# Token mixing by 26 block products on one core: the sums of z a product ahead of their high parts, weight parts four steps ahead in five buffers, gates and biases moved forward

## The chip, the cores and the metric

The kernel runs on one core of a Trainium2 chip. A core has a matrix engine (PE, with weight loads shown apart as PEld), a vector engine (DVE), an activation engine (ACT), a general engine (POOL) and a queue that issues the transfers here (SP). Each engine works through its own list of instructions in order, and waits by semaphores for the others. The metric is the device time of one execution in microseconds (us).

## The reference, cut to what matters

A block of attention is followed by a gated MLP whose gate mixes the 2048 tokens with a 2048 x 2048 matrix. The change lies in the second part:

```python
h = _layernorm(x, axis=-1) * (1 + cb) + sb
z = _gelu(jnp.einsum("bsd,df->bsf", h, w_in))
z1 = z[..., :Fh]
z2 = _layernorm(z[..., Fh:], axis=-1)
g = jnp.einsum("ts,bsf->btf", w_sp, z2) + b_sp[None, :, None]
x = x + gb * jnp.einsum("bsf,fd->bsd", z1 * g, w_out)
```

There are 2048 tokens, 448 channels, and 896 features in each of z1 and z2. Everything is float32.

## The kernel before, in words

The stages follow each other: queries, keys and values; attention over 16 heads; the output projection; z1 and z2; the mixing (the einsum with w_sp); and the last projection with w_out. A float32 product is made of three PE passes on float32r operands: each operand is split into a high part (a copy with rounding, on ACT) and a low part (operand minus high part, on DVE), and high times high, high times low and low times high are summed in PSUM.

**Mixing.** z2 lies in SBUF as four groups of tokens, each with two halves of the features: B is the first 384, A the other 512 (384 and 128). w_sp transposed is cut into 4 x 4 blocks of 512 x 512. In place of 32 block products there are 26 (the table PRODUCTS), each of a sum of z blocks with a sum of weight blocks; its result is added to or subtracted from the output tiles that its row of signs names. Sixteen products are 512 features wide, ten are 384 wide (flag `six`). A product n has four steps (n, 0) to (n, 3), one for each 128 tokens of its group; the list `mix` has the 104 steps. `mix_step` issues 12 matmuls a step for a wide product and 9 for a narrow one, all with 512 columns. Products with even n accumulate in one set of PSUM banks, odd ones in the other.

Around the matmuls each engine has work, and the loop at the end of the function sets its order, step by step:

- `w_load` (SP): brings the raw weight block of a step, 128 x 512, into a tile `raw_sp`. The sums of blocks were made during the attention and lie in DRAM (`ws_scr`); twelve loads come straight from the input.
- `w_split`: the weight's high part `wsp_h` (ACT) and low part `wsp_l` (DVE) of step i + 3, at the start of step i. `raw_sp`, `wsp_h` and `wsp_l` have four buffers each, so the high part of step i + 3 takes the buffer that step i - 1 has used.
- `z_begin(n + 2)` in step (n, 1): the sum of z blocks for product n + 2 (DVE, `z_op`), where there is one, and then its high part (ACT, `z_hi`). `z_end(n + 2)` in step (n, 3): its low part (DVE, `z_low`). The parts lie in `heapA`, in three buffers.
- `read_list(n - 1)`: when product n - 1 is done, its banks are added into the output tiles cE, cC, cF and cD (group k = 0 to 3, tile f = 0 to 6 of 128 features each), at most three at a step: DVE adds, or an ACT copy for the first one of a tile.
- `extra`: work placed by hand with `put` and `gates`. `bias` adds b_sp (POOL), `z1_load` brings a tile of z1 (SP, two buffers), `gate` multiplies by it (POOL; DVE for a few later), `u_split` splits a finished tile for the last projection (ACT and DVE). `wout_load` (SP, two buffers `raw_out`), and `wout_part` (POOL, then ACT and DVE) prepare w_out. `x2_load` brings rows for the last sum.

After the last step come 16 calls of `y_part`, each with 21 matmuls with 448 columns: the last projection.

In the trace, instructions of the shared helper `sub` have line 141, reads, biases and gates (`d_add`) line 1392, the matmuls of the mixing line 1384, weight loads line 1164, z1 loads line 1424 and w_out loads line 1442. The name z stands for z2 and for z1's tiles, cD and so on for the output tiles.

## Time and profile before

| | us |
|---|---|
| median of 3 runs | 1406.65 (1404.82 to 1407.26) |
| the profiled execution's own time | 1407.99 |
| its span, first to last instruction | 1406.1 |
| first and last matmul of the mixing start at | 1050.7 and 1334.1 |
| PE busy, share of the span | 98% |

The 1.9 us between the span and the execution's own time lie outside the instructions. A matmul's record is longer than the time by which the next one follows it, because matmuls are pipelined; so PE reads as busy even where it is slowed, and the number of matmuls that start in a stretch tells more than the share of busy time. The mixing has 1128 matmuls: 420 in products 0 to 9, 528 in products 10 to 21, 180 in products 22 to 25.

### The profile page before, as it was taken

Reading aid. Unit: us, or ns where it says so; the run is one execution under the profiler, and the core shown is the slowest. Engines: PE = TensorE matmul, PEld = TensorE weight load, DVE = VectorE, ACT = ScalarE, POOL = GpSimd, SP = SyncE. Lnnn points to the kernel's source line nnn. Section 1 sums busy time; section 2 is a strip of 40 time slices with the busy share of each in tenths; the row PEclk is TensorE's granted clock in tenths of the full one; section 3 lists DMA queues with packets and bytes.
Section 4 is the critical chain, followed back from the end, with each engine's and each line's share of the span. In section 5 each row is a group of like instructions: output and inputs, shape, how many; then the busy total and the mean of one; then the engine's idle time right before and its main releaser. Section 6 shows DMA issues by size and latency. Waiting matters only on the chain. (4 is left out here: it accounts for less than half of the span.)

```text
span 1406.1 us, 20080 instructions
## 1 busy us (share of the span) xinstructions
PE 1384.8 (98%) x7120; PEld 978.5 (70%) x7120; DVE 1073.5 (76%) x1685; ACT 785.3 (56%) x1458; POOL 427.2 (30%) x394
## 2 busy tenths in 40 slices
PE   9999999999999999999999999999999999998899
PEld 8888655555555555555555556988987788776698
DVE  7798888888888888888888842840477689889661
ACT  5623677666777777666777787452235543343230
POOL 2234334233345336434510021100240014136600
PEclk9999999999999999999999999999999999999999
DMA  8564642455244543553233002532003333344442
GB/s 268 144 178 177 183 123 79 116 161 160 63 121 129 165 113 119 156 147 85 98 98 81 17 22 81 191 126 104 28 9 120 105 111 121 120 128 143 149 149 92
DMA packets 89008, 168.12 MB, mean 120 GB/s; under 512 B 16584, under 2 KB 27978, under 8 KB 86362
## 3 DMA queue, kind: packets, MB, share of 16 engines
q1 hardware_dynamic: 86190, 162.54, 38.5%
q10 hardware_dynamic: 2718, 4.30, 0.8%
q8 instruction: 56, 0.92, 0.3%
q14 instruction: 44, 0.36, 0.1%
HBM read 108.40 MB, written 53.60 MB: 115 GB/s over the span
## 5 line engine op out<-in xcount | busy, mean ns | idle before, releaser
L696 DVE TENSOR_REDUCE pm<-mt 128x1 f32<-128x512 f32 x1024 | 631.7, 682 | 86.1 <-PE mt L691 86.0
L727 ACT ACTIVATE P<-st_ps 128x512 f32<-128x512 f32 x1024 | 514.5, 627 | 201.2 <-PE st_ps L723 201.1
L723 PE MATMUL st_ps<-qst,kst 128*128 128x512 f32 x1024 | 404.3, 406 | 0.0
L691 PE MATMUL mt<-kst,qst 128*128 128x512 f32 x1024 | 402.0, 393 | 0.5 <-DMA qst<-qk_scr 0.5
L723 PEld LDWEIGHTS st_ps<-qst,kst 128*128 128x128 f32 x1024 | 191.2, 188 | 140.3 <-issue 93.1
L738 PE MATMUL o_ps<-P,V 128*32 128x512 f32 x2048 | 247.1, 598 | 0.0
L1384 PE MATMUL acc<-wsp_h,heapA 128*128 128x512 f32 x752 | 239.4, 397 | 6.9 <-ACT wsp_h L1170 3.5
L845 POOL TENSOR_TENSOR ws_raw<-ws_raw 128x512 f32<-128x512 f32 x124 | 159.2, 1287 | 192.8 <-DMA ws_scr<-ws_raw 128.6
L691 PEld LDWEIGHTS mt<-kst,qst 128*128 128x128 f32 x1024 | 192.4, 188 | 33.8 <-issue 0.9
L1384 PEld LDWEIGHTS acc<-wsp_h,heapA 128*128 128x128 f32 x752 | 143.3, 191 | 42.3 <-ACT wsp_h L1170 7.0
L1384 PE MATMUL acc<-wsp_l,heapA 128*128 128x512 f32 x376 | 150.0, 399 | 7.9 <-DVE wsp_l L141 7.8
L738 PEld LDWEIGHTS o_ps<-P,V 128*32 128x32 f32 x2048 | 54.7, 109 | 121.7 <-issue 113.7
L141 DVE TENSOR_TENSOR wsp_l<-raw_sp,wsp_h 128x512 fp32r<-128x512 f32 x104 | 88.1, 864 | 47.0 <-ACT wsp_h L1170 47.0
L1170 ACT ACTIVATE wsp_h<-raw_sp 128x512 fp32r<-128x512 f32 x104 | 62.0, 627 | 77.1 <-PE acc L1384 43.7
L1384 PEld LDWEIGHTS acc<-wsp_l,heapA 128*128 128x128 f32 x376 | 71.8, 191 | 28.3 <-DVE wsp_l L141 14.0
L1203 ACT ACTIVATE heapA<-z 128x1536 fp32r<-128x1536 f32 (+2 forms) x25 | 33.7, 1359 | 54.9 <-DVE z L1193 53.3
L380 PE MATMUL pq<-heapD,heapD 128*128 128x512 f32 x196 | 61.9, 390 | 0.0
L767 POOL TENSOR_TENSOR osb<-osb,rb 128x512 f32<-128x512 f32 x15 | 19.3, 1288 | 122.1 <-DMA rb<-r_scr 112.4
L1282 DVE BATCH_NORM_STATS2 stz<-z 128x6 f32<-128x448 f32 x32 | 20.0, 626 | 46.3 <-ACT z L1281 25.9
L1281 ACT ACTIVATE z<-z_ps 128x448 f32<-128x448 f32 x32 | 17.4, 545 | 47.2 <-PE z_ps L1278 47.2
L1392 POOL TENSOR_TENSOR cE<-cE,bt 128x512 f32<-128x512 f32 x7 | 12.2, 1767 | 99.1 <-DVE cE L1392 99.1
L141 DVE TENSOR_TENSOR heapA<-z,heapA 128x1536 fp32r<-128x1536 f32 (+2 forms) x25 | 42.0, 1689 | 0.0
(219 smaller groups left out, 1520.4 us busy)
## 6 DMA issues: line engine op xcount, KB each, us to landing
ws_scr<-ws_raw SPq DMA_DIRECT2D x92, 256.0 KB
raw_sp<-ws_scr SPq DMA_DIRECT2D x92, 256.0 KB
ws_raw<-in_w_spT_dram SPq DMA_DIRECT2D x72, 256.0 KB
kst<-qk_scr SPq DMA_DIRECT2D x45, 224.0 KB
qst<-qk_scr SPq DMA_DIRECT2D x45, 224.0 KB
qk_scr<-qh SPq DMA_DIRECT2D x28, 256.0 KB
qk_scr<-ql SPq DMA_DIRECT2D x28, 256.0 KB
z_scr<-z1t SPq DMA_DIRECT2D x28, 256.0 KB
```

The lines of the kernel that those rows point to most:

```text
L141: eng.tensor_tensor(out=dst, in0=a, in1=hi.bitcast(F32), op=ALU.subtract)
L380: pe.matmul(pq, wqk[:, b, m * 128 : (m + 1) * 128], hT[g][:, a, :], start=j == 0, stop=j == NST - 1)
L691: pe.matmul(mt, qst[h % 3][:, t * 128 : (t + 1) * 128], kst[h % 3][:, kb * 512 : (kb + 1) * 512], start=True, stop=True)
L696: dve.tensor_reduce(out=pms[h][:, t, kb : kb + 1], in_=mt, axis=AX.X, op=ALU.max)
L723: pe.matmul(st, kst[h % 3][:, kt * 128 : (kt + 1) * 128], qst[h % 3][:, qb * 512 : (qb + 1) * 512], start=True, stop=True)
L727: act.activation(p, st, AF.Exp, scale=SCALE)
L738: pe.matmul(otile[h][32 * qb : 32 * qb + 32, :], V[:, kt, h, :], ptiles.pop((u, qb)), start=kt == 0, stop=kt == NT - 1)
L845: pool.tensor_tensor(out=ws_tile(op[0]), in0=ws_tile(op[2]), in1=ws_tile(op[4]), op=ALU.add if op[3] == "+" else ALU.subtract)
L1170: act.activation(hi, raw, AF.Copy)
L1203: act.activation(zhi[n % 3][:, :, c], s, AF.Copy)
L1282: dve.bn_stats(out=st[:, hf, :], in_=z2[t][:, hf * D : (hf + 1) * D])
L1384: pe.matmul(a[j], z[:, c], w, start=start and k == 0, stop=st == 3 and k == 2, skip_group_check=not new or j == 3)
```

## The change

Seven things are changed, all in the mixing; the arithmetic and the number of instructions of each kind stay.

1. `z_begin` is taken apart. The sum for product n + 3 (`z_sums`) is made in step (n, 3), the high part of product n + 2 (`z_his`) in step (n, 1), its low part (`z_los`) in step (n, 2). Before, sum and high part were made in (n, 1), the low part in (n, 3).
2. `w_split` is taken apart. In step i, `w_hi(i + 4)` comes first on ACT, and `w_lo(i + 4)` comes last on DVE, behind the reads, the z work and the extras of the step. `wsp_h` and `wsp_l` get five buffers, `raw_sp` keeps four. `w_load(i + 6)` stands in place of i + 5. Four steps are ready before the mixing begins, before it three.
3. Two of the sums made by `put` stand two or three steps earlier.
4. The biases are moved forward: group 3 from products 14 to 15 to products 13 to 14, group 2 from 18 and 22 to 15 and 16, group 1 from 20 and 24 to 17 and 18, and their loads with them.
5. The gates of group 1 move from product 25 to 24; those of group 0, tiles 3 to 6, stand two steps earlier, those of tiles 0 to 2 about a step earlier or later. The splits of group 3's tiles 0 to 2 move from product 22 to 21.
6. z1 of group 3, tiles 3 to 6, and the rows of w_out get a tile `late_in` with four places in the old `heapB`; before, they shared pools with two buffers.
7. The rows of w_out are loaded from (23, 0) to (24, 3) in place of (22, 1) to (24, 1); `wout_part` runs from (23, 3) to (25, 1) in place of (23, 1) to (25, 1).

The order of instructions on DVE, where the program makes the sum of product 17 (`zt_sum`), in products 14 to 16; heapA rows are low parts of z, cF rows are reads. Before:

```order
L141 TENSOR_TENSOR wsp_l<-raw_sp,wsp_h 128x512
L1392 TENSOR_TENSOR cF<-cF,acc 128x512 x3
L141 TENSOR_TENSOR wsp_l<-raw_sp,wsp_h 128x512
L1193 TENSOR_TENSOR zt_sum<-zt_sum,z_10936 128x4x384
L1392 TENSOR_TENSOR cF<-cF,acc 128x512
L141 TENSOR_TENSOR wsp_l<-raw_sp,wsp_h 128x512 x2
L141 TENSOR_TENSOR heapA<-zt_sum,heapA 128x4x384
L141 TENSOR_TENSOR heapA<-z_10936,heapA 128x4x128
L141 TENSOR_TENSOR wsp_l<-raw_sp,wsp_h 128x512
L1392 TENSOR_TENSOR cF<-cF,acc 128x512 x3
```

With the change:

```order
L141 TENSOR_TENSOR wsp_l<-raw_sp,wsp_h 128x512
L1194 TENSOR_TENSOR zt_sum<-zt_sum,z_10936 128x4x384
L141 TENSOR_TENSOR wsp_l<-raw_sp,wsp_h 128x512
L1397 TENSOR_TENSOR cF<-cF,acc 128x512 x3
L141 TENSOR_TENSOR wsp_l<-raw_sp,wsp_h 128x512
L1397 TENSOR_TENSOR cF<-cF,acc 128x512
L141 TENSOR_TENSOR wsp_l<-raw_sp,wsp_h 128x512
L141 TENSOR_TENSOR heapA<-zt_sum,heapA 128x4x384
L141 TENSOR_TENSOR heapA<-z_10936,heapA 128x4x128
L141 TENSOR_TENSOR wsp_l<-raw_sp,wsp_h 128x512 x2
```

The sum stands before the three reads in place of behind them, the low part of z a step earlier, and the weight's low parts stand at the end of the steps. On ACT the high part of `zt_sum` keeps its place among the high parts of the weights.

SP's transfers in products 22 to 24 (z_ rows are z1 tiles, raw_sp the weights of the mixing, raw_out and late_in the rows of w_out or z1). Before:

```order
L1442 DMA raw_out<-in_w_out_dram 128x448
L1164 DMA raw_sp<-ws_scr 128x512
L1442 DMA raw_out<-in_w_out_dram 128x448
L1164 DMA raw_sp<-ws_scr 128x512
L1424 DMA z_13374<-z_scr 128x512
L1164 DMA raw_sp<-ws_scr 128x512
L1424 DMA z_13398<-z_scr 128x512
L1442 DMA raw_out<-in_w_out_dram 128x448
L1164 DMA raw_sp<-ws_scr 128x512
L1424 DMA z_13423<-z_scr 128x512
L1442 DMA raw_out<-in_w_out_dram 128x448
L1164 DMA raw_sp<-ws_scr 128x512
```

With the change:

```order
L1164 DMA raw_sp<-ws_scr 128x512
L1436 DMA z_13403<-z_scr 128x512
L1454 DMA late_in<-in_w_out_dram 128x448
L1164 DMA raw_sp<-ws_scr 128x512
L1454 DMA late_in<-in_w_out_dram 128x448
L1164 DMA raw_sp<-ws_scr 128x512
L1436 DMA z_13453<-z_scr 128x512
L1454 DMA late_in<-in_w_out_dram 128x448
L1164 DMA raw_sp<-ws_scr 128x512
L1436 DMA z_13477<-z_scr 128x512
L1454 DMA late_in<-in_w_out_dram 128x448
L1164 DMA raw_sp<-ws_scr 128x512
```

Before, the rows of w_out share two buffers, and the third one stands ahead of a weight load; now they go to four places, later in the list, with a weight load between each two of them.

The diff:

```diff
--- before.py
+++ after.py
@@ -1157,20 +1157,21 @@
     raws, wsp = {}, {}
 
     def w_load(i):
-        if i < len(mix) and i not in raws and i not in wsp:
+        if i < len(mix):
             n, st = mix[i]
             raws[i] = wp.tile([128, 512], F32, name="raw_sp")
             b = PRODUCTS[n][3]
             sp.dma_start(raws[i], ws_scr[4 * n + st] if b is None else w_block(b, st))
 
-    def w_split(i):
-        if i < len(mix) and i not in wsp:
-            raw = raws.pop(i)
-            hi = wp.tile([128, 512], F32R, name="wsp_h")
-            act.activation(hi, raw, AF.Copy)
-            lo = wp.tile([128, 512], F32R, name="wsp_l")
-            sub(dve, lo, raw, hi)
-            wsp[i] = (hi, lo)
+    def w_hi(i):
+        if i < len(mix):
+            wsp[i] = [wp.tile([128, 512], F32R, name="wsp_h", bufs=5)]
+            act.activation(wsp[i][0], raws[i], AF.Copy)
+
+    def w_lo(i):
+        if i < len(mix):
+            wsp[i].append(wp.tile([128, 512], F32R, name="wsp_l", bufs=5))
+            sub(dve, wsp[i][1], raws.pop(i), wsp[i][0])
 
     zt = [dpool.tile([128, 8 * 896], F32, name=f"z2{i}", tag=f"heapD{i}") for i in range(2)]
     z2 = [zt[i // 8][:, i % 8 * FH : (i % 8 + 1) * FH] for i in range(NT)]
@@ -1255,13 +1256,15 @@
         24: lambda: [(C3, ZB[1])],
     }
 
-    def z_begin(n):
+    def z_sums(n):
         for s in SUMS[n]() if n in SUMS else ():
             z_op(*s)
+
+    def z_his(n):
         if n in HIS:
             z_hi(n, *HIS[n]())
 
-    def z_end(n):
+    def z_los(n):
         if n in HIS:
             z_low(n)
 
@@ -1291,15 +1294,15 @@
         dve.tensor_scalar(out=z2[t], in0=z2[t], scalar1=mv[:, 0:1], scalar2=rs, op0=ALU.subtract, op1=ALU.mult)
 
     early_z = {
-        5: lambda: z_begin(0),
-        6: lambda: z_end(0),
+        5: lambda: z_his(0),
+        6: lambda: z_los(0),
         8: zt_new,
         9: lambda: z_op(ZT[0], ZT[0], ZB[0]),
         10: lambda: z_op(ZT[0], ZT[0], ZB[1]),
-        11: lambda: z_begin(1),
-        12: lambda: z_begin(2),
-        13: lambda: z_end(2),
-        14: lambda: z_end(1),
+        11: lambda: z_his(1),
+        12: lambda: z_los(1),
+        13: lambda: z_his(2),
+        14: lambda: z_los(2),
         15: lambda: z_op(ZT[0], ZB[1], ZB[2]),
     }
     for t in range(NT + 1):
@@ -1307,10 +1310,12 @@
             z2_gemm(t)
         if 0 < t <= NT:
             z2_norm(t - 1)
-        if t in (10, 11, 13, 15):
-            w_load((10, 11, 13, 15).index(t))
-        if t in (13, 15, 16):
-            w_split((13, 15, 16).index(t))
+        if 9 <= t < 13:
+            w_load(t - 9)
+        if 12 <= t < 16:
+            w_hi(t - 12)
+        if 13 <= t < 17:
+            w_lo(t - 13)
         if t in early_z:
             early_z[t]()
     ph4.close()
@@ -1410,17 +1415,24 @@
         else:
             d_add(u, u, a, ALU.add if r > 0 else SUB)
 
-    bt, z1s = {}, {}
+    bt, z1s, ring2 = {}, {}, []
 
     def b_load(k):
         bt[k] = t4.tile([128, 512], F32, name="bt")
         sp.dma_start(bt[k], b_sp[k * 512 : (k + 1) * 512].rearrange("(o n) -> o n", o=1).broadcast_to([128, 512]))
 
-    def z1_load(f, k, late=False):
-        if late:
+    def late_tile(i):
+        if not ring2:
+            ring2.append(fh.tile([128, 4, 512], F32, name="late_in", tag="heapB"))
+        return ring2[0][:, i, :]
+
+    def z1_load(f, k, late=0):
+        if late == 0:
+            z1s[f, k] = t4.tile([128, 512], F32, name="z1")
+        elif late == 1:
+            z1s[f, k] = late_tile(f - 3)
+        else:
             z1s[f, k] = wp.tile([128, 512], F32, name="z1l", tag="raw_sp")
-        else:
-            z1s[f, k] = t4.tile([128, 512], F32, name="z1")
         sp.dma_start(z1s[f, k], z1_scr[f * 128 : (f + 1) * 128, k * 512 : (k + 1) * 512])
 
     def bias(f, k, eng=pool):
@@ -1438,7 +1450,7 @@
     x2t = {}
 
     def wout_load(f):
-        x2t["w", f] = raw = t4.tile([128, D], F32, name="raw_out", tag="x2t")
+        x2t["w", f] = raw = late_tile(f % 4)[:, :D]
         sp.dma_start(raw, w_out[f * 128 : (f + 1) * 128, :])
 
     def wout_part(f):
@@ -1451,7 +1463,7 @@
         sub(dve, wouts[1][:, f, :], raw, wouts[0][:, f, :])
 
     def x2_load(t):
-        x2t[t] = wp.tile([128, 512], F32, name="x2l", tag="wsp_l")[:, :D]
+        x2t[t] = wp.tile([128, 512], F32, name="x2l", tag="wsp_l", bufs=5)[:, :D]
         sp.dma_start(x2t[t], x2_scr[t * 128 : (t + 1) * 128, :])
 
     def y_part(t):
@@ -1470,68 +1482,72 @@
     def put(n, st, fn, *a):
         extra.setdefault((n, st), []).append((fn, a))
 
+    def spread(n, st, fs, what, *a, step=1):
+        for i, f in enumerate(fs):
+            put(n + (st + i * step) // 4, (st + i * step) % 4, what, f, *a)
+
     put(0, 1, z_op, ZB[2], ZB[2], ZB[3])
     put(0, 2, z_op, ZAF[2], ZAF[2], ZAF[3])
     put(1, 0, z_op, ZAF[0], ZAF[0], ZAF[2])
-    put(8, 3, z_op, ZAF[0], ZAF[0], ZAF[2], SUB)
     put(5, 3, z_op, ZB[0], ZB[0], ZB[1])
-    put(16, 2, z_op, ZAF[2], ZAF[2], ZAF[3], SUB)
+    put(8, 0, z_op, ZAF[0], ZAF[0], ZAF[2], SUB)
+    put(16, 0, z_op, ZAF[2], ZAF[2], ZAF[3], SUB)
 
     B3, A4 = (0, 1, 2), (3, 4, 5, 6)
     put(8, 0, b_load, 0)
     put(9, 0, b_load, 3)
-
-    def gates(n, st, fs, k, what, **kw):
-        for i, f in enumerate(fs):
-            put(n + (st + i) // 4, (st + i) % 4, what, f, k, **kw) if not kw else put(n + (st + i) // 4, (st + i) % 4, lambda f=f: what(f, k, **kw))
-
-    gates(10, 0, B3, 0, bias)
-    gates(10, 0, B3, 0, z1_load)
-    gates(10, 3, B3, 0, gate)
-    gates(12, 0, A4, 0, bias)
-    gates(14, 0, A4, 3, bias)
-    gates(15, 0, B3, 3, bias)
-    put(16, 2, b_load, 2)
-    put(16, 3, b_load, 1)
-    gates(18, 0, B3, 2, bias)
-    gates(18, 0, B3, 2, z1_load)
-    gates(18, 3, B3, 2, gate)
-    gates(20, 0, B3, 1, bias)
-    gates(20, 0, B3, 3, z1_load)
-    gates(20, 3, B3, 3, gate)
-    gates(21, 1, A4, 3, z1_load)
-    gates(22, 0, A4, 3, gate)
-    gates(22, 1, B3, 3, u_split)
-    gates(22, 3, A4, 0, z1_load)
-    gates(23, 2, A4, 0, gate)
-    gates(23, 0, A4, 3, u_split)
-    gates(22, 0, A4, 2, bias)
-    gates(24, 0, A4, 1, bias)
-    gates(24, 0, A4, 1, z1_load)
-    gates(25, 0, A4, 1, gate)
-    for f in range(7):
-        put(22 + (f + 1) // 3, (f + 1) % 3, wout_load, f)
-        put(23 + f // 3, f % 3 + 1, wout_part, f)
+    spread(10, 0, B3, bias, 0)
+    spread(10, 1, B3, z1_load, 0)
+    spread(11, 0, B3, gate, 0)
+    spread(12, 0, A4, bias, 0)
+    put(13, 1, b_load, 2)
+    spread(13, 0, A4, bias, 3)
+    spread(14, 0, B3, bias, 3)
+    put(15, 0, b_load, 1)
+    spread(15, 0, B3, bias, 2)
+    spread(16, 0, A4, bias, 2)
+    spread(17, 0, A4, bias, 1)
+    spread(18, 0, B3, bias, 1)
+    spread(18, 1, B3, z1_load, 2)
+    spread(19, 0, B3, gate, 2)
+    spread(19, 3, B3, z1_load, 3)
+    spread(20, 2, B3, gate, 3)
+    spread(21, 0, B3, u_split, 3)
+    spread(21, 1, A4, z1_load, 3, 1)
+    spread(22, 0, A4, gate, 3)
+    spread(22, 1, A4, z1_load, 0)
+    spread(23, 0, A4, gate, 0)
+    spread(23, 0, A4, u_split, 3)
+    spread(23, 2, A4, z1_load, 1)
+    spread(24, 0, A4, gate, 1)
+    spread(23, 0, range(4), wout_load)
+    spread(23, 3, range(4), wout_part)
+    spread(24, 1, range(4, 7), wout_load)
+    spread(24, 3, range(4, 7), wout_part)
     for t in range(12, 15):
         put(25, t - 12, x2_load, t)
 
     todo = []
+    w_load(4)
+    w_load(5)
     for i, (n, st) in enumerate(mix):
-        w_load(i + 5)
-        w_load(i + 4)
-        w_split(i + 3 if i else 3)
+        w_load(i + 6)
+        w_hi(i + 4)
         if st == 0 and n:
             todo += read_list(n - 1)
         mix_step(i)
-        if st == 1:
-            z_begin(n + 2) if n + 2 not in (2,) else None
+        if st == 1 and n:
+            z_his(n + 2)
         for _ in range(3):
             if todo:
                 read(*todo.pop(0))
-        if st == 3:
-            z_end(n + 2) if n + 2 not in (2,) else None
+        if st == 2 and n:
+            z_los(n + 2)
         for fn, a in extra.pop((n, st), []):
             fn(*a)
+        if st == 3:
+            z_sums(n + 3)
+        w_lo(i + 4)
     for r in read_list(NP - 1):
         read(*r)
     assert not extra and not todo and len(written) == 28
@@ -1540,9 +1556,9 @@
     banks[:] = order
     last = [12, 13, 14, 15] + list(range(12))
     rest = {
-        0: [(z1_load, f, 1, True) for f in B3] + [(u_split, f, 0) for f in B3 + A4] + [(gate, f, 1, dve) for f in B3],
+        0: [(z1_load, f, 1, 2) for f in B3] + [(u_split, f, 0) for f in B3 + A4] + [(gate, f, 1, dve) for f in B3],
         2: [(u_split, f, 1) for f in A4 + B3],
-        3: [(z1_load, f, 2, True) for f in A4],
+        3: [(z1_load, f, 2, 2) for f in A4],
         4: [(gate, f, 2, dve) for f in A4],
         6: [(u_split, f, 2) for f in A4 + B3],
     }
```

## Prediction

> **What bounds the kernel now.** The change touches only the mixing, so I first asked how much of its time is not matmul work. The stall-free stretch from 1102 to 1152 us gives the pace, the tile view the first and last start (columns: duration ns min/median/max).
>
> ```profile
> 1102.00:1152.00 50.00, 50.00 (x222) 41.41 (x221) 5.81 (x9) 5.58 (x11) 0.00 (x0) 1.00 0.34 107
> L1384 PE MATMUL acc<-wsp_h,heapA x752: 387/389/632, 1050.7 to 1334.1; 128*128 128x512 f32 x188
> L1384 PE MATMUL acc<-wsp_l,heapA x376: 387/389/796, 1050.9 to 1333.9; 128*128 128x512 f32 x188
> ```
>
> A window counts every matmul that touches it, and each is 0.389 us long, so 222 follow each other in 50.39 us: 0.227 us each. All 1128 (752 and 376) need 256.1 us; from 1050.7 to 1334.1, with 0.2 for the last, they took 283.6. So 27.5 us can be won, 2% of the kernel. Where they lie, the windows by product say (0 to 9, 10 to 21, 22 to 25):
>
> ```profile
> core 0: us, PE busy (x) PEld busy (x) DVE busy (x) ACT busy (x) POOL busy (x), PEclk, DMA share, GB/s
> 1050.70:1152.60 101.90, 98.98 (x422) 79.28 (x421) 75.24 (x82) 51.06 (x81) 5.50 (x6) 0.98 0.35 108
> 1152.60:1279.60 127.00, 122.77 (x530) 98.48 (x529) 113.90 (x122) 48.81 (x64) 50.08 (x30) 1.00 0.42 130
> 1279.60:1334.50 54.90, 47.29 (x182) 35.35 (x181) 40.83 (x45) 19.14 (x31) 34.91 (x25) 0.94 0.43 137
> ```
>
> In the same way 422 matmuls at 0.227 in 102.3 us leave 6.5 us lost in the first stretch, 530 leave 7.1 in the second, 182 leave 14.0 in the third: 27.6 together. In the second, DVE is busy for 113.9 of 127.0 us, which will matter. The waits name the culprits (total, times, longest):
>
> ```profile
> ACT heapA L1203 <- DVE z L1193: 53.3, 8, 10.3
> ACT heapA L1203 <- DVE cE L1193: 14.9, 4, 5.2
> ACT heapA L1203 <- DVE zt_sum L1193: 6.7, 1, 6.7
> ACT wsp_h L1170 <- PE acc L1384: 43.7, 29, 2.1
> DVE wsp_l L141 <- ACT wsp_h L1170: 47.0, 27, 4.0
> SPq L1442 <- DVE wouts L141: 20.8, 5, 8.9
> ```
>
> Two mechanisms show in the timeline. The first, around 1213 us:
>
> ```profile
> 1213.09 1.75 DVE L1193 TENSOR_TENSOR zt_sum<-zt_sum,z 128x1536 f32<-128x1536 f32 x1
> 1214.88 1.49 ACT L1203 ACTIVATE heapA<-zt_sum 128x1536 fp32r<-128x1536 f32 x1 [6.74 <-DVE zt_sum L1193]
> 1216.79 2.17 ACT L1170 ACTIVATE wsp_h<-raw_sp 128x512 fp32r<-128x512 f32 x4
> 1217.44 1.29 DVE L141 TENSOR_TENSOR wsp_l<-raw_sp,wsp_h 128x512 fp32r<-128x512 f32 x2 [1.99 <-ACT wsp_h L1170]
> 1217.46 0.50 PE L1384 MATMUL acc<-wsp_h,heapA 128*128 128x512 f32 x1 [0.99 <-ACT wsp_h L1170]
> ```
>
> DVE makes a sum for a product two ahead. ACT, in order, stands 6.74 us before the high part of that sum, while four high parts of weights queue behind it; DVE then waits 1.99 us for the first of these, and PE for both. Nobody needed that sum yet. The second, at the end:
>
> ```profile
> 1298.66 0.38 SPq L1424 DMA_DIRECT2D z<-z_scr  x1
> 1308.02 0.33 SPq L1442 DMA_DIRECT2D raw_out<-in_w_out_dram  x1
> 1308.40 0.42 SPq L1164 DMA_DIRECT2D raw_sp<-ws_scr  x1
> 1311.35 0.63 ACT L1170 ACTIVATE wsp_h<-raw_sp 128x512 fp32r<-128x512 f32 x1 [7.09 <-DMA raw_sp<-ws_scr]
> 1312.01 0.69 DVE L141 TENSOR_TENSOR wsp_l<-raw_sp,wsp_h 128x512 fp32r<-128x512 f32 x1 [2.28 <-ACT wsp_h L1170]
> ```
>
> SP stands from 1298.7 to 1308.0 before the third row of w_out, whose buffer (one of two) frees with DVE's first `wouts`; behind it stands a weight load, for which ACT waits 7.09 us. These stalls have a cost on top:
>
> ```profile
> 1080.00:1100.00 20.00, 18.15 (x68) 12.97 (x67) 13.14 (x17) 14.15 (x25) 0.00 (x0) 0.91 0.28 93
> PE acc L1384 <- ACT cF L1409: 1.6, 1, 1.6
> L1409 ACT ACTIVATE cC<-acc x7: 580/600/647, 1072.2 to 1091.2; 128x512 f32<-128x512 f32 x7
> ```
>
> There PE waits 1.6 us for a read on ACT, yet 68 matmuls in 20.4 us are 22 short of the pace, 5.0 us, since the granted clock falls too (0.91). My 27.6 us hold both.
>
> **The change part by part.** Nothing is added or removed; 104 weight splits, 25 z parts, 28 biases and the rest only move. So the sum is 27.6 minus what stays.
>
> *Products 0 to 9 (6.5 lost).* ACT carries 8 first copies in product 2 and 6 in product 3, and in between waited for sums in cE (14.9 us in the row above). These sums now stand a product earlier, so ACT only has work: by rows of 0.55 for a weight's high part (2.17 for four), 1.49 for z and 0.6 for a copy some 8.5 us in product 2 and 8 in product 3, against 16.3 us of PE. That fits with about 1 us to spare. With a fourth step split before the start, the low parts of steps 1 and 2 that came late move ahead. Bounds: 0 to 2 stay; I take 0.7, near the lower end, since no wait is left between DVE and ACT there.
>
> *Products 10 to 21 (7.1 lost).* Here the ping-pong goes but DVE stays nearly full, and POOL's moved work slows it. Rows of this stretch alone, mean ns behind the bar:
>
> ```profile
> L141 DVE TENSOR_TENSOR wsp_l<-raw_sp,wsp_h 128x512 fp32r<-128x512 f32 x48 | 43.7, 926 | 13.1 <-ACT wsp_h L1170 13.1
> L141 DVE TENSOR_TENSOR heapA<-z,heapA 128x1536 fp32r<-128x1536 f32 x6 | 12.7, 2114 | 0.0
> L1193 DVE TENSOR_TENSOR z<-z 128x1536 f32<-128x1536 f32 x2 | 4.6, 2294 | 0.0
> L1193 DVE TENSOR_TENSOR z<-z,z 128x1536 f32<-128x1536 f32 x2 | 4.6, 2293 | 0.0
> L1193 DVE TENSOR_TENSOR z<-z,z 128x2048 f32<-128x2048 f32 x1 | 3.4, 3373 | 0.0
> L1193 DVE TENSOR_TENSOR z<-z 128x2048 f32<-128x2048 f32 x1 | 2.3, 2284 | 0.0
> L1193 DVE TENSOR_TENSOR zt_sum<-zt_sum,z 128x1536 f32<-128x1536 f32 x1 | 1.8, 1754 | 0.0
> L1392 DVE TENSOR_TENSOR cC<-cC,acc 128x512 f32<-128x512 f32 x14 | 9.0, 677 | 0.0
> ```
>
> A low part alone takes 690 ns (the row at 1312.01), here 926: 48 x 0.236 = 11.3 us. The wide z rows add 6 x 0.36, 4 x 0.54 and 1.09, 5.4 together: 16.7 us over 30 POOL instructions, **0.56 us of DVE for each POOL instruction**. Reads from PSUM keep 677. By the program 37 biases and gates now fall into these products, 29 before; one sum (1.67) and three splits for the last projection (1.8) come in too. DVE then needs 113.9 + 8 x 0.56 + 3.5 = 121.9 us, PE 528 x 0.227 = 119.9. DVE may fall behind by the lead of the weights, three narrow steps of 9 x 0.227, 6.1 us, before PE waits; the 2.0 fit, and so does the worst product, 18 (7 reads and 4 low parts at 0.6, as two low parts in 1.29 us follow each other above; two z operations of 1.67 + 0.6; 3 x 0.56: 12.8 us against PE's 8.2). The 13.1 us that DVE waited for ACT are what becomes free. One POOL instruction can cost from nothing (beside reads) to 1.09 us (3373 less 2284). At 1.09, DVE needs 113.9 + 3.5 + 8 x 1.09 + 30 x 0.53 = 142.0, 22.1 too many, 16 past the lead. Bounds 0 to 16; I take 1.0, by the mean.
>
> The Trainium skill, page "SBUF — State Buffer", section "Who interferes with whom", says that a DVE instruction with two inputs in SBUF and a GpSimd instruction that reads SBUF contend for a shared port, an exclusive lock, while one SBUF input does not. The trace agrees on who is slowed; By a full block, 1.3 us of POOL for three quarters of DVE's time, the 37 would cost 36 us in place of 21 and the end come 10 us later than by my sum; that is the first rival below.
>
> *Products 22 to 25 (14.0 lost).* The rows of w_out get four places, and they and z1 of group 3 no longer share two buffers, so the 8.9 us stop of SP goes. What is late next: the last five low parts of weights stand on DVE behind `wouts`, which waits for ACT, POOL and the z1 pairs ahead of it on POOL.
>
> ```profile
> 1308.93 4.68 DMA z<-z_scr
> 1326.08 3.60 DMA raw_sp<-ws_scr
> L1392 POOL TENSOR_TENSOR cD<-cD,z 128x512 f32<-128x512 f32 x7 | 13.7, 1957 | 21.2 <-DMA z<-z_scr 19.4 <-DVE cD L1392 1.2 <-DVE wsp_l L141 0.6
> 1319.64 1.15 POOL L1392 TENSOR_TENSOR raw_out<-raw_out,bc_gb 128x448 f32<-128x448 f32 x1
> ```
>
> Counted from the start of product 22: the first gate of group 0 at 8 us (load in step 1, 4.7 landing), then eight gates in pairs, each pair waiting 4.7 us for its reload, with w_out rows between them, at 1.2 to 2.0 us each. The fifth w_out row is through POOL at about 8 + 8 x 1.6 + 5 x 1.3 + 3 x 2.2 (what POOL's own work leaves uncovered of three reloads) = 34 us; ACT, `wouts` and the last low part add 2; PE needs it at 10.9 + 10.9 + 8.2 and three wide steps, 38. So it fits by 2 us. Bounds 0 (all early) to 8 (each POOL instruction at 1.96, 6 us more, and a reload of 4.7 behind one of them); I take 1.8.
>
> The last projection keeps its order. **Sum:** 0.7 + 1.0 + 1.8 = 3.5 stay, 24.1 are won. From the profiled span of 1406.1 to 1382.0, with the 1.9 around it 1383.9; the profiled run lay 1.3 above the median of the runs, so **1382.6 us** from 1406.65.
>
> **The rivals.**
> *DVE becomes the bound in products 10 to 21*, slowed by POOL's forward work. For it: 113.9 of 127.0 us busy. Against: the mean is 0.56. At 0.8 each it needs 131, 5 past the lead, at 1.09 it is 16: 1386.6 to 1397.6, say 1392.
> *The end keeps its stall in a new form*, the POOL chain: 8 us in place of 1.8, 1389. For it: only 2 us to spare; against: weight loads no longer stand behind a shared pair.
> *Slower: the ring of raw weights.* `raw_sp` keeps four buffers, and what frees one, the low part, now stands last in its step. If the work did not overlap, a ring of four steps would hold SP 0.4, landing 4.7, ACT 0.6, three reads 1.9, two sums 3.5, the low part 0.7: 11.8 us against 8.2 for a narrow product and 10.9 for a wide one. Then 10 x 3.6 + 16 x 0.9 = 50 us are lost where 27.6 are won: 1429. It decides once the ring passes 8.2 us. Against: reads and sums run while the load is under way, which leaves 6.4.
> *It does not do what it says*: with five buffers the high part of step i + 4 waits for step i - 1, as that of i + 3 did with four, so the 43.7 us wait of ACT stays, and if that wait is what paces the stage, time stays within 0.2%, 1406.
>
> **How the numbers follow.** Forecast 0.57, DVE bound 0.20, end chain 0.13, ring 0.05, nothing 0.05. A measurement tells about 0.2% (2.8 us) from no change. Faster 0.57 + 0.20 + 0.13 = 0.90, same 0.05, slower 0.05. All 27.6 gone is 1379.1, and the fastest run lay 1.8 under the median: low 1377.5. High 1396, most of the DVE rival's way.
>
> **What would show it.** Right: ACT waits for sums of z nearly gone; DVE's idle time before `wsp_l` in the middle below 5 us; no stop of SP at w_out rows; about 180 matmuls in some 42 us at the end. DVE-bound: DVE without idle time from product 12 on, and PE waiting for `wsp_l` or for a read at product 19. The forecast is wrong if PE still loses over 10 us in any stretch, or ACT waits for raw weights throughout.

## The result, and the profile after

| | before | after |
|---|---|---|
| median of the runs beside each other, us | 1406.95 | 1386.09 (1383.94 to 1387.48) |
| ratio to before, 95% interval | | 0.9853 (0.9836 to 0.9870) |
| the profiled execution's time and span | 1407.99, 1406.1 | 1386.58, 1384.8 |
| first and last matmul of the mixing start at | 1050.7, 1334.1 | 1050.0, 1312.8 |

The change wins 20.9 us, where 24.1 were forecast (1382.6). In the profiled executions the mixing is 20.6 us shorter; the other 0.7 of the 21.3 us between their spans lie ahead of it, where the start of the first matmul varies by up to 1.5 us among the kernels below. The windows by product, in the same three stretches as before (0 to 9, 10 to 21, 22 to 25; columns: window, length, then busy time and count on PE, PEld, DVE, ACT and POOL, the granted clock, DMA share, GB/s):

```profile
1050.00:1145.20 95.20, 95.20 (x422) 78.84 (x420) 81.42 (x88) 53.78 (x83) 6.17 (x5) 1.00 0.38 118
1145.20:1268.30 123.10, 120.46 (x530) 98.89 (x529) 122.68 (x120) 52.29 (x66) 62.22 (x35) 1.00 0.41 128
1268.30:1313.00 44.70, 41.99 (x181) 33.46 (x180) 44.70 (x41) 14.66 (x24) 28.49 (x18) 1.00 0.59 186
```

The first stretch now takes 95.2 us for its 420 matmuls, 0.2267 us each, and no kernel below does it faster. Counted at this pace from the first matmul of a stretch to the first of the next, the first stretch loses nothing, the second (528 matmuls) 3.4 us and the third (180) 3.9. The kernel before lost 6.7, 7.3 and 14.0 by the same count; the prediction, with 0.227, had 6.5, 7.1 and 14.0. The granted clock is 1.00 in every stretch, where it was 0.98, 1.00 and 0.94. But DVE is now busy almost without a gap from 1145 to the end of the mixing: 122.68 us of 123.1, then 44.70 of 44.70. The waits of the whole mixing (total, times, longest) show the same turn:

```profile
ACT heapA L1204 <- DVE z L1194: 7.4, 2, 4.2
ACT heapA L1204 <- DVE zt_sum L1194: 1.7, 1, 1.7
DVE wsp_l L141 <- ACT wsp_h L1169: 7.2, 9, 2.0
SPq L1454 <- DVE wouts L141: 2.8, 1, 2.8
ACT wsp_h L1169 <- PE acc L1389: 75.2, 46, 2.1
ACT wsp_h L1169 <- DMA raw_sp<-ws_scr: 26.3, 14, 4.5
PE acc L1389 <- DVE wsp_l L141: 5.2, 4, 1.7
```

ACT waited 74.9 us for sums of z, in rows that now read 7.4 and 1.7. DVE waited 47.0 for ACT and now waits 7.2. SP stood 20.8 us before rows of w_out and now stands 2.8. What PE still waits for is one thing, a weight's low part that DVE has not made yet. The four waits are 5.2 us; counted from one matmul's start to the next, five gaps, four of them these waits, hold 6.1 of the 7.3 us, and the rest lies in matmuls that follow a little more slowly. Two places carry the losses. The first lies in products 15 to 17, in the timeline:

```profile
1199.95 7.47 POOL L1397 TENSOR_TENSOR cF<-cF,bt 128x512 f32<-128x512 f32 x4 [4.10 <-DVE cF L1397]
1203.43 2.84 DVE L141 TENSOR_TENSOR heapA<-zt_sum,heapA 128x1536 fp32r<-128x1536 f32 x1
1206.19 1.78 DVE L141 TENSOR_TENSOR heapA<-z,heapA 128x512 fp32r<-128x512 f32 x1
1207.39 6.36 POOL L1397 TENSOR_TENSOR cC<-cC,bt 128x512 f32<-128x512 f32 x4
1207.90 3.44 DVE L141 TENSOR_TENSOR wsp_l<-raw_sp,wsp_h 128x512 fp32r<-128x512 f32 x2
1209.71 0.50 PE L1389 MATMUL acc<-wsp_l,heapA 128*128 128x512 f32 x1 [1.56 <-DVE wsp_l L141]
```

POOL had waited 4.10 us for a read of DVE, and then eight biases follow each other for 13.8 us. Beside them DVE's low part of zt_sum takes 2.84 us and each low part of a weight 1.72; PE runs dry at 1209.7. The second place is the end:

```profile
1294.44 1.59 POOL L1397 TENSOR_TENSOR late_in<-late_in,bc_gb 128x448 f32<-128x448 f32 x1
1294.94 1.57 DVE L141 TENSOR_TENSOR wouts<-late_in,wouts 128x448 fp32r<-128x448 f32 x1
1295.99 1.65 POOL L1397 TENSOR_TENSOR cC<-cC,z 128x512 f32<-128x512 f32 x1
1296.44 1.75 DVE L141 TENSOR_TENSOR wsp_l<-raw_sp,wsp_h 128x512 fp32r<-128x512 f32 x1
1297.60 1.59 POOL L1397 TENSOR_TENSOR late_in<-late_in,bc_gb 128x448 f32<-128x448 f32 x1
1298.11 1.57 DVE L141 TENSOR_TENSOR wouts<-late_in,wouts 128x448 fp32r<-128x448 f32 x1
1298.24 0.50 PE L1389 MATMUL acc<-wsp_l,heapA 128*128 128x512 f32 x1 [1.69 <-DVE wsp_l L141]
1301.43 0.50 PE L1389 MATMUL acc<-wsp_l,heapA 128*128 128x512 f32 x1 [0.85 <-DVE wsp_l L141]
```

Both engines work without a gap, starting in turn, and an instruction of either takes about 1.6 us; before, such a low part of a weight took 0.69 where it ran alone. From 1294.94 to 1298.11 DVE gets through one row of w_out and one weight, 3.2 us, while PE uses up a step in 2.0 (nine matmuls) or 2.7 (twelve).

### The profile page after: what moved, and what is told of

Same layout as the page of the kernel before. It is cut to its first block, busy times and chain, and to the rows that moved or that the text cites. A ratio compares the mean times of both kernels' runs of the same rounds, so it can differ in the third digit from the quotient of the medians.

```text
span 1384.8 us, 20104 instructions
## 1 busy us (share of the span) xinstructions
PE 1374.8 (99%) x7120; PEld 977.7 (71%) x7120; DVE 1091.8 (79%) x1685; ACT 787.9 (57%) x1458; POOL 433.6 (31%) x394
## 4 chain that ended last, share of the span: by engine, by line
PE 92%; DVE 5%; issue 2%; DMA 0%; ACT 0%; DVEq 0%
PE st_ps L723 19%; PE o_ps L738 17%; PE mt L691 17%; PE acc L1389 11%; PE z_ps L1281 5%; PE pq L380 5%; PE z_ps L1113 5%; PE wo_ps L979 3%; DVE wsp_l L141 2%; PE pv L362 2%; PE y_ps L1473 2%; PE y_ps L1474 2%; PE y_ps L1475 2%; PE tp L174 1%; PE wu L287 1%
## 5 line engine op out<-in xcount | busy, mean ns | idle before, releaser
L1389 PE MATMUL acc<-wsp_h,heapA 128*128 128x512 f32 x752 | 231.8, 389 | 0.0
L1389 PE MATMUL acc<-wsp_l,heapA 128*128 128x512 f32 x376 | 147.1, 391 | 5.4 <-DVE wsp_l L141 5.2
L1169 ACT ACTIVATE wsp_h<-raw_sp 128x512 fp32r<-128x512 f32 x104 | 65.3, 631 | 114.2 <-PE acc L1389 75.2
L141 DVE TENSOR_TENSOR wsp_l<-raw_sp,wsp_h 128x512 fp32r<-128x512 f32 x104 | 95.2, 932 | 7.3 <-ACT wsp_h L1169 7.2
L767 POOL TENSOR_TENSOR osb<-osb,rb 128x512 f32<-128x512 f32 x15 | 19.3, 1290 | 121.4 <-DMA rb<-r_scr 118.1
L141 DVE TENSOR_TENSOR heapA<-z,heapA 128x1536 fp32r<-128x1536 f32 (+2 forms) x25 | 49.4, 1987 | 1.8 <-ACT heapA L1204 1.8
L705 POOL TENSOR_SCALAR mxv<-mxv 128x16 f32<-128x16 f32 x16 | 4.1, 254 | 123.5 <-DVE mxv L703 123.5
L380 PEld LDWEIGHTS pq<-heapD,heapD 128*128 128x128 f32 x196 | 36.7, 188 | 7.5
```

The lines of the kernel that those rows point to most:

```text
L141: eng.tensor_tensor(out=dst, in0=a, in1=hi.bitcast(F32), op=ALU.subtract)
L380: pe.matmul(pq, wqk[:, b, m * 128 : (m + 1) * 128], hT[g][:, a, :], start=j == 0, stop=j == NST - 1)
L1169: act.activation(wsp[i][0], raws[i], AF.Copy)
L1389: pe.matmul(a[j], z[:, c], w, start=start and k == 0, stop=st == 3 and k == 2, skip_group_check=not new or j == 3)
```

## The experiments

Three questions stood open after that: is it POOL that makes DVE full; which part of the change won what; and could any of the rivals still be at work?

### POOL beside DVE

Five kernels leave the change as it is and alter only the 28 biases, or what else POOL does. By the program all biases stand in products 10 to 21; on POOL three of them run at 1136 to 1141 us, just before PE starts product 10.

**Biases left out.**

```diff
     def bias(f, k, eng=pool):
-        d_add(utile(f, k), utile(f, k), bt[k], eng=eng)
+        pass
```

> The changed kernel without its 28 bias additions on POOL (b_sp is not added; everything else stays). Theory 'price': the 7.3 us that PE still loses come from POOL instructions that slow DVE by 0.8 us each in products 9 to 21; without 28 of them DVE has idle time again there, the 3.3 us lost in products 16 and 17 go, and the end, entered without a backlog, loses 1 to 4 in place of 3.9: 1380 to 1383 us. Rival 'chain': the losses come from raw weights that land late behind their four buffers, whatever DVE has to do: 1385 to 1387.

Measured: 1380.74 us, ratio to before 0.9822 (0.9807 to 0.9836). The middle loses nothing and the end 0.9. So the biases cost the changed kernel about 5 us (5.3 by the medians, 4.4 by the ratios to before).

**Biases on DVE.**

```diff
-    def bias(f, k, eng=pool):
+    def bias(f, k, eng=dve):
```

> The changed kernel with the 28 bias additions on DVE in the same places. Theory 'price': a bias costs DVE 0.61 us as its own instruction and 0.8 as a neighbour on POOL, so DVE gains 28 x 0.2 = 5 us and PE loses 0 to 2 us in products 10 to 21 in place of 3.3: 1382 to 1385. Rival 'chain': DVE gets 17 us more work ahead of the low parts, 1387 to 1395.

Measured: 1382.13 us, ratio 0.9829 (0.9814 to 0.9844): DVE does 28 instructions more, and the kernel is 4.0 us shorter. The middle loses nothing, the end 3.0.

**A fill in place of a bias.**

```diff
-        d_add(utile(f, k), utile(f, k), bt[k], eng=eng)
+        eng.memset(utile(f, k), 0.0)
```

> The changed kernel with each of the 28 biases on POOL replaced by a fill of the same tile with zeros, at the same place and with the same waits: b_sp and what was summed in the tile before are left out of the result. POOL then writes and reads nothing. If POOL slows DVE because both read SBUF, the price is gone although POOL works in the same places: 1380 to 1382, as with the biases left out (1380.7), and DVE busy for about 106 us in products 10 to 21. If any work of POOL in SBUF slows DVE, or if the waits between DVE and POOL for the output tiles cost the time, it stays at 1385 to 1387. The Trainium skill, page "SBUF - State Buffer", section "Who interferes with whom", gives the first answer.

Measured: 1380.23 us, ratio 0.9817 (0.9801 to 0.9833). (A fill still writes the tile; it reads nothing.)

**A multiplication by 1.0 in place of a bias.**

```diff
-        d_add(utile(f, k), utile(f, k), bt[k], eng=eng)
+        eng.tensor_scalar(out=utile(f, k), in0=utile(f, k), scalar1=1.0, scalar2=None, op0=ALU.mult)
```

> The changed kernel with each of the 28 biases on POOL replaced by a multiplication of the tile by 1.0: one read of 128x512 in place of two, one write, the same places and waits; b_sp is left out of the result. If each POOL instruction costs DVE a fixed price as soon as it reads SBUF, 1385 to 1387, as the changed kernel. If the price goes with what POOL reads, half of the 5.3 us between the changed kernel and the one without biases is won: 1383 to 1384. If only POOL instructions with two inputs slow DVE, 1380 to 1382.

Measured: 1381.47 us, ratio 0.9826 (0.9811 to 0.9841). This is below the 1383 to 1384 of the middle case and as good as no price; but a price that fits into DVE's idle time does not show in the kernel's time, only in the table below.

**All of POOL's work on DVE.**

```diff
-    def bias(f, k, eng=pool):
+    def bias(f, k, eng=dve):
...
-    def gate(f, k, eng=pool):
+    def gate(f, k, eng=dve):
...
-        d_add(raw, raw, bcs["gb"], ALU.mult, eng=pool)
+        d_add(raw, raw, bcs["gb"], ALU.mult, eng=dve)
```

> The changed kernel with every bias, every gate of the mixing and the multiplications of w_out on DVE, so that POOL does nothing in the mixing. If DVE's time is what remains to be won, the gates cost DVE 0.6 us each there and 0.81 us or more beside it on POOL: 1380 to 1382, no slower than the version with biases and w_out on DVE (1381.9). If the waits of gates for their transfers of z1 (about 4.7 us each) then stop DVE, PE loses 5 to 10 us in the last four products: 1385 to 1390.

Measured: 1381.35 us (1381.03 to 1381.91), ratio 0.9827 (0.9812 to 0.9841). The gates' waits for z1 did not stop DVE: the end loses 1.7.

What decides shows in the windows of products 10 to 21 (columns as above). With fills:

```profile
1145.70:1265.40 119.70, 119.70 (x530) 99.11 (x529) 106.34 (x121) 52.40 (x66) 30.24 (x36) 1.00 0.44 134
```

With the multiplications by 1.0:

```profile
1145.20:1264.90 119.70, 119.70 (x530) 99.15 (x529) 111.44 (x121) 52.42 (x66) 63.62 (x36) 1.00 0.43 134
```

With the biases left out:

```profile
1145.80:1265.50 119.70, 119.70 (x530) 99.11 (x529) 105.88 (x121) 52.39 (x66) 16.91 (x11) 1.00 0.45 134
```

With the biases on DVE:

```profile
1146.40:1266.10 119.70, 119.70 (x530) 99.12 (x529) 119.27 (x148) 52.30 (x66) 18.08 (x11) 1.00 0.42 130
```

All four run at PE's pace, 119.7 us, against 123.1 with biases on POOL. DVE's busy time over that without biases, divided by the number of biases that run in the stretch (25 on POOL, 28 on DVE), is the price of one:

| in place of a bias, 128x512 | DVE busy, us | price for DVE, us each | POOL busy, us |
|---|---|---|---|
| left out | 105.88 | | 16.91 |
| fill, reads nothing | 106.34 | 0.02 | 30.24 |
| times 1.0, reads one tile | 111.44 | 0.22 | 63.62 |
| bias, reads two tiles | 122.68 of 123.1 | at least 0.67 | 62.22 |
| bias on DVE itself | 119.27 of 119.7 | at least 0.48 | 18.08 |

"At least", since DVE has no more time to give there. So it is not how long POOL works that costs DVE: the one-tile form keeps POOL as busy as the bias and costs a third. It is what POOL reads; whether the number of inputs counts or the kind of operation that comes with it, these runs do not separate. Nor are the waits for the output tiles to blame, since the fill and the one-tile form keep them. The groups of DVE's operations in the same window agree. In the changed kernel (mean ns behind the bar):

```profile
L141 DVE TENSOR_TENSOR wsp_l<-raw_sp,wsp_h 128x512 fp32r<-128x512 f32 x46 | 46.1, 1019 | 0.4 <-ACT wsp_h L1169 0.4
L141 DVE TENSOR_TENSOR heapA<-z,heapA 128x2048 fp32r<-128x2048 f32 x6 | 15.2, 2533 | 0.0
L141 DVE TENSOR_TENSOR heapA<-z,heapA 128x1536 fp32r<-128x1536 f32 x5 | 12.5, 2504 | 0.0
L141 DVE TENSOR_TENSOR heapA<-z,heapA 128x512 fp32r<-128x512 f32 x3 | 5.3, 1778 | 0.0
L1397 DVE TENSOR_TENSOR cD<-cD,acc 128x512 f32<-128x512 f32 x18 | 11.7, 674 | 0.0
```

With POOL idle (all on DVE, the same window of that run):

```profile
L141 DVE TENSOR_TENSOR wsp_l<-raw_sp,wsp_h 128x512 fp32r<-128x512 f32 x47 | 31.8, 680 | 0.9 <-ACT wsp_h L1169 0.9
L141 DVE TENSOR_TENSOR heapA<-z,heapA 128x2048 fp32r<-128x2048 f32 x6 | 13.7, 2280 | 0.0
L141 DVE TENSOR_TENSOR heapA<-z,heapA 128x1536 fp32r<-128x1536 f32 x5 | 8.7, 1749 | 0.3 <-ACT heapA L1204 0.3
L141 DVE TENSOR_TENSOR heapA<-z,heapA 128x512 fp32r<-128x512 f32 x3 | 2.0, 677 | 0.0
L1397 DVE TENSOR_TENSOR cD<-cD,bt 128x512 f32<-128x512 f32 x7 | 4.8, 680 | 0.0
```

A low part goes from 680 ns to 1019, while a read from PSUM (`cD<-cD,acc`) stays at 674. The four differences, 46 x 0.339, 6 x 0.253, 5 x 0.755 and 3 x 1.101, make 24.2 us. Five sums and low parts in smaller groups (that of zt_sum went from 1.74 us to the 2.84 shown above) add 3.8: 28.0 us over 35 POOL instructions, 0.80 each. A bias on DVE takes 680 ns, part of which the next instruction overlaps, and raised DVE's busy time by 0.48 in the table. So in this stretch the kernel lost less by keeping the biases on DVE: 28 instructions more there, and PE loses 3.4 us less. The Trainium skill, page "SBUF — State Buffer", section "Who interferes with whom", says that a DVE instruction with two inputs in SBUF contends with a GpSimd instruction that reads SBUF, not with one that only writes. The fill's 0.02 against the bias's 0.67 agrees.

### Which part won what

**The sums alone.** The kernel before, with parts 1 and 3 of the change.

```diff
-        if st == 1:
-            z_begin(n + 2) if n + 2 not in (2,) else None
+        if st == 1 and n:
+            z_begin(n + 2)
...
-        if st == 3:
-            z_end(n + 2) if n + 2 not in (2,) else None
+        if st == 2 and n:
+            z_end(n + 2)
...
+        if st == 3:
+            z_sums(n + 3)
```

> The kernel before with the first and third part of the change alone (sums of z a product ahead, high and low parts a step apart, two sums moved). If the wait of ACT for sums is what cost the first stretch, products 0 to 9 lose 1 to 3 us in place of 6.5, products 10 to 21 lose 2 to 5 in place of 7.1, the end keeps its 14: 1396 to 1400 us. If the lead of four steps is what matters, little moves: 1404 to 1407.

Measured: 1391.54 us, ratio 0.9898 (0.9881 to 0.9915), by the ratio about 14.3 us less: more than either theory gave. Of the losses, 1.7, 0.8 and 8.8 remain in the three stretches; the 1.7 are all in product 0, where part 2 takes them away. The windows of the last two:

```profile
1147.20:1267.70 120.50, 120.14 (x529) 98.97 (x528) 115.07 (x120) 50.91 (x63) 50.01 (x30) 1.00 0.45 133
1267.70:1317.30 49.60, 43.66 (x182) 33.25 (x181) 40.10 (x43) 16.74 (x28) 36.26 (x23) 1.00 0.45 139
```

The middle is better than in the full change (0.8 against 3.4), since the biases still stand where they were (the run below with the biases back has the same 0.8), and the end also gains 5.2 us although only the z parts of its last two products were moved.

**The places of w_out alone.** The kernel before, with `late_in` for w_out and for z1 of group 3, and the new times of the w_out rows (parts 6 and 7).

```diff
-        x2t["w", f] = raw = t4.tile([128, D], F32, name="raw_out", tag="x2t")
+        x2t["w", f] = raw = late_tile(f % 4)[:, :D]
...
-    gates(21, 1, A4, 3, z1_load)
+    gates(21, 1, A4, 3, z1_load, late=1)
...
-    for f in range(7):
-        put(22 + (f + 1) // 3, (f + 1) % 3, wout_load, f)
-        put(23 + f // 3, f % 3 + 1, wout_part, f)
+    for f in range(4):
+        put(23, f, wout_load, f)
+        put(23 + (3 + f) // 4, (3 + f) % 4, wout_part, f)
+    for f in range(4, 7):
+        put(24, f - 3, wout_load, f)
+        put(24 + (f - 1) // 4, (f - 1) % 4, wout_part, f)
```

> The kernel before with the four places for w_out's rows and group 3's z1, and w_out's later times, alone. If the stop of SP behind the third row of w_out is what cost the end, products 22 to 25 lose 4 to 7 us in place of 14, the rest stays: 1396 to 1400 us. If the end is paced by POOL and DVE in any case: 1403 to 1407.

Measured: 1406.02 us, ratio 0.9996 (0.9986 to 1.0005): no difference. The mixing does end 4.2 us earlier in the profile. Of these, 1.3 lie in products 0 to 9, which the edit does not touch; the end loses 11.1 in place of 14.0. But the last projection takes 2.5 us longer and gives most of that back. Its rows on SP, and then the chain of waits (start, us, engine, tile), say how:

```profile
1321.43 0.32 SPq L1431 DMA_DIRECT2D z<-z_scr  x1
...
1327.78 0.32 SPq L1431 DMA_DIRECT2D z<-z_scr  x1
1328.15 0.42 SPq L1449 DMA_DIRECT2D late_in<-in_w_out_dram  x1
```

```profile
1332.38 1.17 POOL late_in L1392
...
1333.56 0.58 ACT wouts L1457
...
1334.17 1.09 DVE wouts L141
...
1335.30 0.47 PE y_ps L1470
```

The last row of w_out stands on SP behind a load of z1 that waits, until 1327.8, for a gate of POOL to free its buffer. The row then comes through POOL, ACT and DVE only at 1335.3, where PE is already in the last projection. SP's stop went (its waits before rows of w_out fall from 20.8 us to 2.4), and another took its place in the same queue (10.9 us before loads of z1 that wait for POOL, in place of 3.0). POOL's eight late biases, of group 2 in product 22 and of group 1 in product 24, still stand ahead of these gates; the next run bears on that.

**Biases back.** The changed kernel with the biases and their loads at their old products.

```diff
-    put(13, 1, b_load, 2)
-    spread(13, 0, A4, bias, 3)
-    spread(14, 0, B3, bias, 3)
-    put(15, 0, b_load, 1)
-    spread(15, 0, B3, bias, 2)
-    spread(16, 0, A4, bias, 2)
-    spread(17, 0, A4, bias, 1)
-    spread(18, 0, B3, bias, 1)
+    spread(14, 0, A4, bias, 3)
+    spread(15, 0, B3, bias, 3)
+    put(16, 2, b_load, 2)
+    put(16, 3, b_load, 1)
+    spread(18, 0, B3, bias, 2)
+    spread(20, 0, B3, bias, 1)
+    spread(22, 0, A4, bias, 2)
+    spread(24, 0, A4, bias, 1)
```

> The changed kernel with the biases and their loads at the places that they had before (29 POOL instructions by program in products 10 to 21 in place of 37, 27 in 22 to 25 in place of 19). Theory 'price': products 10 to 21 lose 0 to 1 us in place of 3.4; the end, where POOL now has 8 more, loses 7 to 10 in place of 4.0: 1386 to 1390. If moving the biases costs DVE nothing, 10 to 21 still lose about 3.4.

Measured: 1392.85 us, ratio 0.9899 (0.9883 to 0.9916), above the range I gave: the end was costed too low. The windows of the last two stretches:

```profile
1146.60:1267.10 120.50, 119.97 (x530) 99.05 (x529) 117.03 (x119) 52.28 (x66) 47.94 (x29) 1.00 0.42 129
1267.10:1319.60 52.50, 44.55 (x181) 34.35 (x180) 50.75 (x41) 14.64 (x24) 42.91 (x25) 0.97 0.54 169
```

The middle loses 0.8 in place of 3.4, as expected; the end loses 11.8 in place of 3.9, with 25 POOL instructions there in place of 18. So moving the biases forward costs 2.6 us in the middle and wins 7.8 at the end.

**The lead back.** The changed kernel without part 2: weights split three steps ahead at the start of a step, in four buffers.

```diff
-        w_load(i + 6)
-        w_hi(i + 4)
+        w_load(i + 5)
+        if i + 3 not in wsp and i + 3 < len(mix):
+            w_hi(i + 3)
+            w_lo(i + 3)
...
-        w_lo(i + 4)
```

> The changed kernel without its second part: weight parts of step i + 3 at the start of step i, in four buffers, three steps ready at the start. Theory 'price': DVE's amount of work stays, but its low parts come first in the step, so a backlog hits the reads before the weights; PE waits once the backlog passes two steps and not three: products 10 to 21 lose 3 to 6 us in place of 3.4, the first product loses 1.7 again, the end 4 to 6: 1387 to 1392. If the lead of four steps adds nothing (the high part waits for the same step of PE either way): 1386 to 1388.

Measured: 1391.61 us, ratio 0.9893 (0.9879 to 0.9908): the lead is worth 5.5 us, near the upper end of the first theory's range. The stretches lose 1.7, 6.1 and 2.6; product 16 alone loses 4.5 in place of 1.9. The first is as that theory said and the second at its upper end; for the end it gave 4 to 6, and why 2.6 is less than the 3.9 of the changed kernel stays open.

**Three raw buffers.** The changed kernel with one buffer less for `raw_sp`, the last z1 tiles put into the ring of `wsp_h`, and the fourth load ahead of the mixing moved behind the first low part.

```diff
-            raws[i] = wp.tile([128, 512], F32, name="raw_sp")
+            raws[i] = wp.tile([128, 512], F32, name="raw_sp", bufs=3)
...
-        if 9 <= t < 13:
+        if 9 <= t < 12:
             w_load(t - 9)
...
+        if t == 13:
+            w_load(3)
...
-            z1s[f, k] = wp.tile([128, 512], F32, name="z1l", tag="raw_sp")
+            z1s[f, k] = wp.tile([128, 512], F32, name="z1l", tag="wsp_h", bufs=5)
```

> The changed kernel with three buffers for raw weights in place of four: the ring is one step shorter. If the ring of raw weights paces any product, each of the 26 loses about a step's share, 1 us or more: 1400 us or slower. If it lies beside DVE's work, as forecast, three narrow steps of 2.04 us still cover load, high and low part of 5 to 6 us only just: 1386 to 1392, and ACT waits longer for raw weights than the 32 us of the changed kernel.

Measured: 1389.27 us, ratio 0.9878 (0.9863 to 0.9893). ACT's wait for raw weights, 26.3 us in the changed kernel, becomes (total, times, longest):

```profile
ACT wsp_h L1169 <- DMA raw_sp<-ws_scr: 45.5, 25, 5.6
```

A buffer less costs 3.2 us by the medians, which the noise hardly separates: the intervals of the two ratios overlap. In the profiled executions, 2.5 us apart, 1.6 show in the middle, which loses 5.0 in place of 3.4; the end loses 3.9 as before, and 1.0 lies ahead of the mixing. So the ring does not pace the whole mixing even with three buffers; that theory wanted 1400 and more.

**A version that beats both.** The changed kernel with the biases and the multiplications of w_out on DVE, the gates left on POOL.

```diff
-    def bias(f, k, eng=pool):
+    def bias(f, k, eng=dve):
...
-        d_add(raw, raw, bcs["gb"], ALU.mult, eng=pool)
+        d_add(raw, raw, bcs["gb"], ALU.mult, eng=dve)
```

> The changed kernel with biases and the multiplication of w_out's rows on DVE, in their places. Theory 'price': at the end POOL and DVE take turns, one low part 1.7 us in place of 0.6 beside a multiplication; with the 7 multiplications on DVE (0.54 each) products 22 to 25 lose 0 to 1.5 us in place of 3.1 with the biases alone on DVE, the rest nothing: 1379 to 1381. If the end is paced by transfers of z1 and w_out, it stays at 1382.

Measured: 1381.88 us (1379.66 to 1382.16), ratio 0.9821 (0.9806 to 0.9836): 4.2 us under the changed kernel, and 0.9 above the range of the first theory. By the median it is what the second gave, an end paced by transfers; the profile is for the first, since the stretches lose 0, 0 and 1.5, where the version with only the biases on DVE loses 3.0 at the end. The place at the end that answers to the one shown of the changed kernel:

```profile
1292.49 0.68 DVE L141 TENSOR_TENSOR wsp_l<-raw_sp,wsp_h 128x512 fp32r<-128x512 f32 x1
1293.09 0.61 DVE L1397 TENSOR_TENSOR late_in<-late_in,bc_gb 128x448 f32<-128x448 f32 x1
1294.35 1.00 DVE L141 TENSOR_TENSOR wouts<-late_in,wouts 128x448 fp32r<-128x448 f32 x1 [0.64 <-ACT wouts L1462]
1300.59 0.50 PE L1389 MATMUL acc<-wsp_l,heapA 128*128 128x512 f32 x1 [1.19 <-DVE wsp_l L141]
```

A weight, the multiplication and a row of w_out take 0.68, 0.61 and 1.00 us, 2.3 together; with the wait of 0.64 for ACT the next weight starts 2.8 us after this one. The turns took 3.2 for a weight and a row without the multiplication. This version, the one with only the biases on DVE (1382.13) and the one with all on DVE (1381.35) are not told apart. What costs the last 1.5 us was not pursued.

## Why the prediction was right, and where it was not

**Sign and size.** 20.9 us were won, 24.1 forecast; 7.3 us stay lost where the sum kept 3.5. The parts do not add: alone the sums win 14.3 and the w_out places nothing, while taking the lead out of the whole, or putting the biases back, costs 5.5 or 6.8. No run takes part 5, 6 or 7 out of the whole, and none tests part 5, the gates, at all.

**Products 0 to 9: right.** 0.7 forecast, 0 measured. That ACT stands before a sum nobody needs yet, with weights queued behind it, was the main cause: the sums alone win more than half of all. Their effect at the end (14.0 to 8.8) I had not counted. The step that failed is that I gave each stretch a mechanism of its own.

**Products 10 to 21: the mechanism right, the price too low.** Forecast 1.0, measured 3.4. The sum put 0.56 us of DVE on each POOL instruction and found 2.0 us of excess, less than the lead of 6.1. In the same count it is 0.80 after the change, and 1.07 for a low part of a weight that takes turns with POOL (1.75 less 0.68). At 0.8 the prediction's own working for its first rival has DVE 5 us past the lead, so the step that failed is the term 0.56. The biases also bunch, which a mean over a stretch does not show: they wait for reads, then run back to back, eight in 13.8 us, just where the lead runs out. How much of the 3.4 this adds, no run separates. I had named product 18 as the worst; PE ran dry in 16 and 17. So the first rival, DVE becomes the bound, came true by its own signs, DVE without idle time and PE waiting for `wsp_l`, but 2.4 us above the sum and not the 9 for which its 1392 stood.

**The rule on SBUF.** Weighed against the mean, I let the Trainium skill's page "SBUF — State Buffer", section "Who interferes with whom", change only a rival. The turns of POOL and DVE at the end fit the contention that it describes, and its limit, that a POOL instruction which only writes does not contend, held (0.02 us each). Taken as a full block of DVE by all 37, as the prediction worked it out, it would have put the end 10 us later than my sum, at about 1393; that did not come. The rows show one reason, reads from PSUM that stay at 674 ns; how much of POOL's time falls beside them was not counted.

**Products 22 to 25: right size of the gain, wrong cause.** 12.2 us were to go and 10.1 went, so near the forecast partly by luck. The step that failed is "the 8.9 us stop of SP goes" as the price of the end: with that stop removed and the rows loaded later, and nothing else changed, nothing is won, while the biases that I had costed only in the middle are worth 7.8 us here. That the four places are needed too, since gates and rows of w_out share POOL and SP, is argued and not shown. What stayed, 3.9 in place of 1.8, was not the chain of reloads that I counted (34 us against 38). Part of it is POOL and DVE slowing each other; with biases and multiplications on DVE, 1.5 is left. Part is carried over from the middle: with the biases left out POOL has the same work at the end, and only 0.9 is lost. In the traces the tightest of product 22's four low parts ends 0.5 us before the first matmul that reads it in the changed kernel, and 3.2 us before with the biases left out.

**The other rivals.** The ring of raw weights does not pace, though ACT waits for raw weights 14 times, at up to 4.5 us: PE never waits for a high part, and DVE for only 0.4 us in the middle (its row above). The wait of ACT for PE's buffers indeed stayed (75.2 us in place of 43.7) and paced nothing; with the biases left out, where the mixing is 6.4 us shorter, it is longer still, 100.5. It shows ACT ahead of PE, not PE behind ACT.

**The clock.** The losses held a share of it, as I had read: with most stalls gone the clock reads 1.00 throughout, and in the two versions that still lose over 11 us at the end it reads 0.97 (biases back) and 0.93 (w_out alone). The size of the loss alone does not set it: the sums alone lose 8.8 us at the end at 1.00. The starts of the matmuls give a bound for its share. Gaps of 0.52 us and more between two starts cost 19.3 us over the pace before and 6.1 after; gaps of 0.30 to 0.52, among which slowed matmuls lie beside short waits, cost 7.9 and 0.9. So some 7 of the 20.6 us at most lie in slowed matmuls outside the longer gaps.

## What to carry to other kernels

An engine that works in order should be given nothing before its input is due: move the sum a stage earlier rather than ask the consumer to wait with other work behind it. Before handing elementwise work to POOL beside a full DVE, take the mean time of the same DVE operation with POOL idle and busy: where both read two tiles of SBUF, 680 ns became 1019 here, and keeping the work on DVE was cheaper. Look also at where POOL's work bunches, and test a queue's stop by removing it alone before pricing it.

## What the hardware showed that I had not expected

On POOL, an operation that reads one tile took as long as one that reads two (1.69 to 1.92 us against 1.54 to 1.98, mean by group) but cost DVE 0.22 us in place of at least 0.67. And an engine that was left idle altogether made the kernel faster: POOL's busy time in products 10 to 21 went from 62.22 us to 0, DVE took them over (157 instructions in place of 120), and its own busy time fell from 122.68:

```profile
1146.20:1265.80 119.60, 119.60 (x529) 99.06 (x528) 118.05 (x157) 52.10 (x66) 0.00 (x0) 1.00 0.42 130
```
